# Three start-up edits in a fused attention and SiLU kernel: where a small read is issued, how many warm-up matmuls run, and how a cast is shared

## The chip, the core and the metric

The kernel runs on one core of a Trainium2 chip. A core has five engines that run beside each other: TensorE (PE, matrix products into PSUM), VectorE (DVE), ScalarE (ACT), GpSimd (POOL) and SyncE (SP, which here only issues transfers). Transfers between main memory and the core's SBUF run on 16 DMA engines. They can be issued from SP's queue and ScalarE's queue (hardware queues, q1 and q10 in the profile) and from GpSimd's (the software queue, q0), and only GpSimd's change the element type on the way. The metric is device time in microseconds, the median over runs; lower is better.

## The reference

Inputs are float32. `q`, `k`, `v` have the shape 8 x 8 x 576 x 64 (batch, head, position, feature), `w_in` 512 x 2048 and `w_out` 2048 x 512.

```python
q_s = exp(q - max(q, axis=-1));  q_s /= sum(q_s, axis=-1) + 1e-09     # over features
k_s = exp(k - max(k, axis=2));   k_s /= sum(k_s, axis=2) + 1e-09      # over positions
kv  = einsum('bhsd,bhse->bhde', k_s, v)
x   = einsum('bhsd,bhde->bhse', q_s, kv)      # then heads side by side: 4608 x 512
h   = x @ w_in
out = (h * sigmoid(h)) @ w_out                # 4608 x 512, float32
```

## The kernel before

The 4608 tokens are eight batches of 576 positions. The attention works by batch: q and k go through an exponential on ScalarE, q is divided by its row sums, `kv` is a small product over positions, and `x` is q (transposed) times kv. The two wide products work in chunks of 512 tokens, from chunk 1 on with a scheme that uses seven block products in place of eight. Chunk 0 covers the 576 tokens of batch 0 and is done plainly.

The order of all work is written out by hand. `ORDER` at the top of the file is a list of names; the loop at the end of the kernel calls them one by one, and each engine carries out its own instructions in that order. A scheduler adds the waits that the data need, but moves nothing.

Names that matter here, all in the opening that handles batch 0:

- `touch(i, x, eng)` (line 550) reads 64 single float32 numbers, spread over a large tensor, into a corner of a tile that is used much later. Nothing uses the numbers. It is called for k and v of batch 0 on ScalarE's queue and for `w_in` on GpSimd's (lines 554 to 556), ahead of everything in `ORDER`.
- `heat(n)` (line 561) issues n matmuls of float32 zeros, 128x128 by 128x512, into PSUM bank 5. Nothing uses the result. `heat0` has five and stands ahead of batch 0's first exponential, `heat1` has one and stands between the first transposes (`tr0.0`) and the first kv product (`kv0.0`).
- `lq0.c`, `lk0.c`, `lv0.0`, `lv0.1.g`: the loads of batch 0, on SP. A tile is 128 rows by two heads; half 1 of v comes in two parts, one head pair each.
- `gate` (line 627): a GpSimd copy of one number of k's first tile. Since GpSimd works in order, it holds back what follows, the loads of `w_in`.
- `W1a0`, `W1a1`, `W1b`, `W1c`, `W1d` (line 628, function `load_w1`): `w_in` in four quarters of 512 columns, the first in two parts, float32 to float16 on the way, on GpSimd's queue. `W2a` and so on do the same for `w_out`.
- `eq`, `z`, `n`: exponential, row sum, normalisation of q; `tr`, `tc`: transposes on TensorE and their copies out of PSUM; `ek`: exponential of k; `vc`: cast of v to bfloat16; `kv`, `kc`: the kv product and its normalising copy; `X0.c`, `x0.c`: the product x and its copies out of PSUM.
- `vc0.1a`, `vc0.1b`, `vc0.1c` (line 619): the cast of v's last half for batch 0. GpSimd takes the first part (nine position groups of 64 features); the second part is cut between ScalarE (groups 0 to 4) and VectorE (groups 5 to 8). `kv0.1.1` waits for both.
- `w{f}.0`, `w{f}.1` (line 306): the wide matmuls of chunk 0 for block f of `w_in`'s columns. Blocks 0 to 3 use W1a, blocks 4 to 7 use W1b.

Of the kernel before, what the change touches and what calls it, by code (L numbers as in the profile page):

```python
# [16 lines left out]

ORDER = """
    lq0.0 lq0.1 lk0.0 lv0.0 lk0.1 lv0.1.0 lv0.1.1 gate W1a0 W1a1 W1b W1c heat0 eq0.0.0 z0.0.0 eq0.0.1 z0.0.1 eq0.1
    n0.0 ek0.0 z0.1 tr0.0 vc0.0 heat1 n0.1 tc0.0b kv0.0 tc0.0a kc0.0 tr0.1 ek0.1 vc0.1b X0.0 tc0.1b  # L20
    vc0.1a vc0.1c W1d lq1.0 lq1.1 W2a kv0.1.0 kv0.1.1 kc0.1 tc0.1a x0.0v X0.1 x0.0a x0.1v w0.0 w2.0 w1.0 x0.1a W2b1 lk1.0 w1.1 h1 w0.1 w3.0 w2.1
    W2b2 w3.1 h0 v1 v0 w5.0 w5.1 w4.0 w4.1 h2 v2 h3 w6.0 w6.1 h5 v3 h4 v5 w7.0 w7.1 h7 WS1.1 w9.0 v4 h6 w9.1 WS0.1
    w8.0 w8.1 v7 lk1.1 h9 h8 w11.0 v6 eq1.0.0 w11.1 v9 v8 h11 WS1.2 w10.0 lv1.1 w10.1 v11 w12.0 w12.1 eq1.0.1 W2c1
# [47 lines left out]
def kernel(  # L71
# [9 lines left out]
    nc = tc.nc  # L81
# [4 lines left out]
    J = S // P  # L86
# [463 lines left out]
    def touch(i, x, eng):  # L550
        rows4 = x.rearrange("(a p z) f -> p a z f", a=4, p=16)
        eng.dma_start(out=touched[:, i, :, None], in_=rows4[:, :, 0, 0:1])

    touch(0, k[0].rearrange("h s d -> (h s) d"), nc.scalar)
    touch(1, v[0].rearrange("h s d -> (h s) d"), nc.scalar)
    touch(2, w_in, nc.gpsimd)
    make_identity(nc, ident_f)
    nc.vector.tensor_copy(ident, ident_f)
    nc.vector.memset(vaug[:, :, :, D:E1], 1.0 / XS)
# [24 lines left out]
    def op(name, f, *args):  # L584
        assert name not in ops
        ops[name] = lambda: f(*args)
# [29 lines left out]
    for g in range(2):  # L616
        op(f"lv0.1.{g}", load, 0, "vt", v, 1, nc.sync, g, g + 1)
        op(f"kv0.1.{g}", kv, 0, 1, 6, g, g + 1)
    for x, eng, g, j0, j1 in (("a", nc.scalar, 1, 0, 5), ("b", nc.vector, 1, 5, J), ("c", nc.gpsimd, 0, 0, J)):
        op(f"vc0.1{x}", vcast, 0, 1, eng, g, g + 1, j0, j1)  # L620
    for c, b0, b1 in ((0, 4, 0), (1, 6, 2)):
        op(f"X0.{c}", lambda c=c, b0=b0, b1=b1: (xt_mm(0, c, 0, 320, b0, 0), xt_mm(0, c, 320, 256, b1, 0)))
        op(f"x0.{c}a", xt_evac, 0, c, b0, 0, 320, 0, nc.scalar)
        op(f"x0.{c}v", xt_evac, 0, c, b1, 0, 256, 320, nc.vector)
    for i, n in enumerate((5, 1)):
        op(f"heat{i}", heat, n)
    op("gate", lambda: nc.gpsimd.tensor_copy(gate, st[0]["kt", 0][0:1, 1, 0:1]))
    for x, f, n, c0, c1 in (("W1a0", 0, 4, 0, 2), ("W1a1", 0, 4, 2, 4), ("W1b", 4, 4, 0, 4), ("W1c", 8, 4, 0, 4), ("W1d", 12, 4, 0, 4)):
        op(x, load_w1, f, f + n, c0, c1)
# [67 lines left out]
    for t in range(1, NCH):  # L697
# [6 lines left out]
        for g in range(2):  # L704
            n = f"{t}.{g}."
# [123 lines left out]
```

## Time and profile before

| | |
|---|---|
| median of 3 runs | 256.7 us (256.35 to 260.25) |
| the profiled execution, its own time | 257.51 us |
| its span, first to last instruction | 255.7 us |
| TensorE matmuls busy | 247.9 us, 97% of the span |
| VectorE / ScalarE / GpSimd busy | 205.7 / 190.6 / 66.7 us |
| read from and written to main memory | 36.70 MB and 9.44 MB |
| mean granted TensorE clock | 0.999 of full speed |

All times in the views are microseconds from the start of the span. A row of the order of time gives start, duration, engine, source line, operation, output and inputs with shapes, a count, and in brackets how long the engine sat idle before and what ended that. In the chain that ended last, each row is a start, a duration and what the end was waiting on at that time. In the view of waits a row gives who waited for whom, the total, how often and the longest. A DMA queue's row gives packets, megabytes and the time that its packets took as a share of 16 engines; overlapping packets can bring that over 100%.

### The profile page before, as it was taken

To read this page: it belongs to the slowest core of one execution; us is meant where nothing else is said; L and a number is where in the kernel's file an instruction comes from. 1 tells how busy PE (TensorE), PEld (TensorE's weight loads), DVE (VectorE), ACT (ScalarE), POOL (GpSimd) and SP (SyncE) were. 2 spreads that over 40 slices of the span, in tenths; PEclk is the share of its full clock that TensorE was granted. 3 is DMA by queue.
4 is the path that set the end of the run, shared out by engine and by line. 5 is a ranking of instruction groups with operands and counts; after the bars stand their busy time and mean duration, and the time that the engine had idled before them with its cause. 6 is when DMAs were issued, how large, how long until landed. Compare 5 with 4: busy or idle time off the path is not lost.

```text
span 255.7 us, 6428 instructions
## 1 busy us (share of the span) xinstructions
PE 247.9 (97%) x2712; PEld 204.3 (80%) x2712; DVE 205.7 (80%) x277; ACT 190.6 (75%) x226; POOL 66.7 (26%) x64
## 2 busy tenths in 40 slices
PE   7789999999999999999999999999999999999994
PEld 3367755666888888888888888888888888888883
DVE  3868998899999998998987986896569836886752
ACT  4765867899999999999879979737587666664411
POOL 2563872540360631530083040006000000000022
PEclk9999999999999999999999999999999999999999
DMA  7999999879959947996964950021807000700365
GB/s 231 350 200 298 270 337 328 310 150 382 388 117 242 404 158 181 349 307 165 301 246 87 243 198 3 3 61 24 170 6 160 6 0 4 154 11 3 69 139 124
DMA packets 36205, 45.90 MB, mean 180 GB/s; under 512 B 16448, under 2 KB 21248, under 8 KB 36176
## 3 DMA queue, kind: packets, MB, share of 16 engines
q1 hardware_dynamic: 29424, 33.56, 45.1%
q0 software_dynamic: 6192, 11.60, 17.6%
q10 hardware_dynamic: 560, 0.33, 0.6%
q8 instruction: 21, 0.34, 0.6%
q14 instruction: 8, 0.07, 0.1%
HBM read 36.70 MB, written 9.44 MB: 180 GB/s over the span
## 4 chain that ended last, share of the span: by engine, by line
PE 89%; DMA 7%; DVE 1%; POOL 1%; ACT 1%; SPq 0%; issue 0%; ACTq 0%
PE PS L502 37%; PE PS L424 35%; PE PS L444 5%; PE PS L306 5%; DMA W<-in_moe_w_in_dram 4%; DMA kt<-in_k_dram 3%; PE PS L334 2%; PE PS L247 2%; PE PS L281 2%; DMA out_dram<-ow 1%; POOL W L566 1%; DVE h L144 0%; PE PS L233 0%; SPq L151 0%; DVE ow L763 0%; ACT ow L776 0%
## 5 line engine op out<-in xcount | busy, mean ns | idle before, releaser
L402 DVE TENSOR_TENSOR h<-PS,h 128x1024 f32<-128x1024 f32 (+1 forms) x45 | 54.1, 1205 | 9.5 <-PE PS L424 7.8
L502 PEld LDWEIGHTS <-GT 128*128 128x128 f16 x512 | 50.0, 98 | 6.0
L424 PEld LDWEIGHTS <-WS 128*128 128x128 f16 x480 | 46.6, 98 | 6.8 <-issue 1.0
L408 ACT ACTIVATE GT<-h 128x1024 f16<-128x1024 f32 (+1 forms) x45 | 46.7, 1050 | 0.9 <-DVE h L402 0.8
L502 PE MATMUL PS<-W,GT 128*128 128x256 f16 x384 | 47.2, 273 | 0.0
L424 PE MATMUL PS<-XS,WS 128*128 128x256 f16 (+1 forms) x360 | 45.0, 272 | 0.0
L142 ACT COPY h<-PS 128x1024 f32<-128x1024 f32 (+1 forms) x31 | 31.1, 1003 | 16.9 <-PE PS L424 15.8
L502 PEld LDWEIGHTS <-S 128*128 128x128 f16 x384 | 37.1, 98 | 4.7
L424 PEld LDWEIGHTS <-W 128*128 128x128 f16 x360 | 35.1, 98 | 4.5 <-issue 0.2
L215 POOL TENSOR_TENSOR eq<-eq,rzq 128x1152 bf16<-128x1152 bf16 x13 | 27.7, 2139 | 36.0 <-DVE rzq L210 35.8
L144 POOL CAST vaug<-vt 128x1152 bf16<-128x1152 f32 (+1 forms) x13 | 16.3, 1268 | 61.4 <-DMA vt<-in_v_dram 53.3
L502 PE MATMUL PS<-T,S 128*128 128x256 f16 x256 | 32.0, 273 | 0.0
L424 PE MATMUL PS<-XT,W 128*128 128x256 f16 (+1 forms) x240 | 29.9, 272 | 0.0
L144 DVE COPY h<-PS 128x1024 f32<-128x1024 f32 (+1 forms) x14 | 17.0, 1212 | 8.6 <-PE PS L424 3.7
L162 ACT ACTIVATE eq<-qt 128x1152 bf16<-128x1152 f32 (+1 forms) x19 | 18.8, 1008 | 4.6 <-DMA qt<-in_q_dram 4.6
L781 POOL DMA_DIRECT2D out_dram<-ow x5 | 2.7, 545 | 70.0 <-DVE ow L763 70.0
L167 ACT ACTIVATE ek<-kt 128x1152 bf16<-128x1152 f32 x16 | 18.4, 1161 | 3.3 <-DMA kt<-in_k_dram 3.2
L408 ACT ACTIVATE GT<-PS 128x1024 f16<-128x1024 f32 (+1 forms) x15 | 15.2, 1014 | 6.6 <-PE PS L424 6.5
L206 DVE TENSOR_REDUCE zq<-eq 128x18 f32<-128x1152 bf16 x13 | 17.5, 1346 | 1.2 <-ACT eq L162 0.9
L306 PE MATMUL PS<-XT,W 128*128 128x288 f16 x128 | 16.0, 286 | 0.4 <-DMA W<-in_moe_w_in_dram 0.4
L502 PE MATMUL PS<-T,GT 128*128 128x256 f16 x128 | 16.3, 273 | 0.0
L502 PE MATMUL PS<-W,S 128*128 128x256 f16 x128 | 16.1, 273 | 0.0
(86 smaller groups left out, 332.8 us busy)
## 6 DMA issues: line engine op xcount, KB each, us to landing
out_dram<-ow SPq DMA_DIRECT2D x64, 128.0 KB, 3.3
qt<-in_q_dram SPq DMA_DIRECT2D x12, 576.0 KB, 5.7
kt<-in_k_dram SPq DMA_DIRECT2D x12, 576.0 KB, 7.1
vt<-in_v_dram SPq DMA_DIRECT2D x11, 576.0 KB, 6.9
qt<-in_q_dram POOLq DMA_DIRECT2D x4, 576.0 KB, 11.9
kt<-in_k_dram POOLq DMA_DIRECT2D x4, 576.0 KB, 12.6
vt<-in_v_dram POOLq DMA_DIRECT2D x4, 576.0 KB, 12.1
W<-in_moe_w_in_dram POOLq DMA_DIRECT2D x3, 512.0 KB, 10.4
```

Of the source, the lines that this page charges most:

```text
L142: eng.copy(out=o, in_=i)
L144: eng.tensor_copy(o, i)
L162: nc.scalar.activation(out=half(st[b]["eq"], cc)[:, :, g0:g1], in_=jgd(b, "qt", cc)[:, :, g0:g1], func=ACT.Exp)
L167: nc.scalar.activation(out=half(ek, cc), in_=jgd(b, "kt", cc), func=ACT.Exp)
L206: nc.vector.reduce_sum(out=z, in_=e, axis=AX.X)
L215: eng.tensor_tensor(out=e, in0=e, in1=r[:, :, :, None].to_broadcast([128, J, 2, D]), op=ALU.mult)
L306: nc.tensor.matmul(out=PS[:, WIDE[fb] + n, 0:S // 2], lhsT=W1[:, c, fb * 128:(fb + 1) * 128], rhs=XTS[0][:, c, n * (S // 2):(n + 1) * (S / ...
L402: nc.vector.tensor_tensor(out=four(t, i), in0=group_bank(t, g), in1=four(t, i), op=ALU.add)
L408: nc.scalar.activation(out=group_out(t, f, n), in_=x, func=ACT.Silu, scale=1.0 / XS)
L424: nc.tensor.matmul(out=PS[:, bank + p // 2, (p % 2) * HT:(p % 2) * HT + width(t)], lhsT=a[:, c, p * 128:(p + 1) * 128], rhs=bb[:, c, 0:wid ...
L444: nc.tensor.matmul(out=PS[:, 2 + tb, :], lhsT=GTS[t % 2][:, fc, tb * 128:(tb + 1) * 128], rhs=W2[:, fc, :], start=(fc == 0), stop=(fc == N ...
L502: nc.tensor.matmul(out=PS[:, bank, m * HN:(m + 1) * HN], lhsT=a[:, fc, m * 128:(m + 1) * 128], rhs=bb[:, fc, :], start=(first and fc == 0) ...
```

## The change

Three edits, all in the opening. The small read of `w_in` is issued on ScalarE's queue, as the other two are, and no longer on GpSimd's. `heat0` has three matmuls in place of five, and `heat1` with its one is gone from `ORDER`. Of the last part of v's cast for batch 0, ScalarE takes four position groups in place of five, and VectorE five in place of four.

```diff
-    n0.0 ek0.0 z0.1 tr0.0 vc0.0 heat1 n0.1 tc0.0b kv0.0 tc0.0a kc0.0 tr0.1 ek0.1 vc0.1b X0.0 tc0.1b
+    n0.0 ek0.0 z0.1 tr0.0 vc0.0 n0.1 tc0.0b kv0.0 tc0.0a kc0.0 tr0.1 ek0.1 vc0.1b X0.0 tc0.1b
...
-    touch(2, w_in, nc.gpsimd)
+    touch(2, w_in, nc.scalar)
...
-    for x, eng, g, j0, j1 in (("a", nc.scalar, 1, 0, 5), ("b", nc.vector, 1, 5, J), ("c", nc.gpsimd, 0, 0, J)):
+    for x, eng, g, j0, j1 in (("a", nc.scalar, 1, 0, 4), ("b", nc.vector, 1, 4, J), ("c", nc.gpsimd, 0, 0, J)):
         op(f"vc0.1{x}", vcast, 0, 1, eng, g, g + 1, j0, j1)
...
-    for i, n in enumerate((5, 1)):
-        op(f"heat{i}", heat, n)
+    op("heat0", heat, 3)
```

## The prediction

> **What bounds the kernel now.** I read the chain that ended last first, cut to its first 40 us.
>
> ```profile
> 1.75 6.62 DMA kt<-in_k_dram
> 8.38 0.05 issue
> 8.43 0.18 POOL gate L627
> 8.61 1.43 POOL W L566 x2
> 10.04 9.22 DMA W<-in_moe_w_in_dram
> 19.26 0.05 issue
> 19.31 11.93 PE PS L306 x96
> ```
>
> Until 19.3 us the end is set by transfers. The first k tile lands at 8.38, the gate lets GpSimd issue W1's quarters, and the second quarter (W1b) lands at 19.26. From 19.31 TensorE runs without a hole: the view of waits for TensorE alone names none after that. So whatever moves 19.31 moves the end by as much, and whatever comes earlier counts only if it moves 19.31. TensorE's own order of time shows the opening:
>
> ```profile
> 1.49 6.74 PE L563 MATMUL PS<-h 128*128 128x512 f32 x10 [1.49 <-DVE h L545]
> 8.54 0.66 PE L233 MATMUL PS<-ident,eq 128*128 128x128 bf16 x9 [0.31 <-DVE eq L215]
> 9.04 1.08 PE L563 MATMUL PS<-h 128*128 128x512 f32 x2
> 11.11 0.48 PE L247 MATMUL PS<-vaug,ek 64*64 64x65 bf16 x36 [0.99 <-ACT vaug L142]
> ...
> 12.90 0.95 PE L247 MATMUL PS<-vaug,ek 64*64 64x65 bf16 x36 [0.26 <-POOL vaug L144]
> 14.44 0.44 PE L281 MATMUL PS<-qT,kvn 64*64 64x320 bf16 x8 [0.59 <-DVE kvn L260]
> 14.81 4.09 PE L306 MATMUL PS<-XT,W 128*128 128x288 f16 x32
> 19.31 0.91 PE L306 MATMUL PS<-XT,W 128*128 128x288 f16 x6 [0.40 <-DMA W<-in_moe_w_in_dram]
> ```
>
> Each float32 warm-up matmul is two records, so five are ten. The wide matmuls on W1's first quarter begin at 14.81, end at 18.91, and wait 0.40 for W1b. That 0.40 is the slack in front of all that the change touches.
>
> Last, the small reads, the gate and the last v casts in the order of time of all engines:
>
> ```profile
> 1.33 0.67 POOL L552 DMA_DIRECT2D kvn<-in_moe_w_in_dram  x1 [0.89 <-POOLq L813]
> 1.34 0.43 ACTq L552 DMA_DIRECT2D kvn<-in_v_dram  x1
> ...
> 8.43 0.18 POOL L627 COPY gate<-kt 1x1 f32<-1x1 f32 x1 [5.84 <-DMA kt<-in_k_dram]
> ...
> 12.86 0.47 ACT L142 CAST vaug<-vt 128x320 bf16<-128x320 f32 x1 [0.15 <-DMA vt<-in_v_dram]
> 12.86 0.29 DVE L144 CAST vaug<-vt 128x256 bf16<-128x256 f32 x1 [0.71 <-DMA vt<-in_v_dram]
> ```
>
> **The warm-up.** Three matmuls go, 3 x 2 records. Two follow the third in heat0 (four records of 0.43 us, 6.35 to 8.23); nothing real waits for TensorE before 8.54, where the first transpose waits for VectorE. heat1 fills 9.04 to 10.12, ahead of a 0.99 us wait for ScalarE's cast. Direct gain: 0. What remains is the clock, a rival below. The page's clock row cannot show it (it has no record before the first change); the spacing does: weight loads and records start at 2.50, 3.36, 4.21, 5.06 and 5.92, 0.85 us apart, then at 6.35, 6.78 and 7.21, 0.43 apart. The clock doubled at 5.92, after 4.43 us of unbroken work, inside the third matmul.
>
> **The small read.** GpSimd loses an issue of 0.67 us. Its identity matrix comes 0.67 earlier, but that is first needed at 8.54, and GpSimd then idles 5.84 us before the gate. ScalarE's queue gains a third issue of 0.43 (row at 1.34), ending at about 2.2; its next real work is the first q at 4.57 after 2.33 idle. Hidden, with 1.9 to spare.
>
> Two queues are moved past. The semaphore records show that SP's and ScalarE's transfers share eight completion semaphores in turn, the ninth reusing the first: the last v load waits for the first q tile (landed 4.55). With one more in front, the last but one v load on SP has to wait for that q tile, where it was issued at 3.56, and the last one for the small read of k (landed 4.10) and its turn. That is about 1.0 and 0.4 us later. Their bytes queue behind k's second tile, which lands at 11.38 with the engines full from 3.5 on, so their landings of 12.13 and 12.84 should stand; if not, the first 0.40 is still covered at W1b. GpSimd's transfers have eight of their own: W2's first part no longer follows the small read, and every later pair is the same as before.
>
> What no row shows is W1's first load being the first transfer GpSimd issues at all. From below: 0. From above: the small read was issued at 1.33 and the software queue has no packet before 5.26, 3.93 us; W1's first was issued at 8.55, first packet 11.33, 2.78 us; GpSimd's last stores, into nearly empty engines, took about 1.27 (250.29 to 251.56). So a first use may cost 3.93 - 2.78 = 1.15, at most 3.93 - 1.27 = 2.66. I take 0: the small read's issue of 0.67 is no longer than W1's (0.74 to 0.77), and ScalarE's second read was slow in the same crowd (issued at 1.34, landed at 5.54).
>
> **The v cast.** ScalarE goes from 320 to 256 elements a row. By its rows of 320 (0.468) and 1152 (1.162) an element costs 0.83 ns: 0.415, ending at 13.28 in place of 13.33. VectorE goes from 256 to 320: 0.295 plus 64 elements at 0.5 ns (its 128x128 identity cast took 0.23) to 1.33 ns (512 from PSUM took 0.68): 0.33 to 0.38, ending before 13.24. Behind it VectorE's transpose copy slides 0.09 at most, and VectorE then idles 0.40 before the reciprocal at 13.89. So kv's second half, X0.1 and the wide matmuls come 0.05 earlier (14.76).
>
> **Sum.** W1b still lands at 19.26; the 0.05 lengthens its wait to 0.45. Total 0.0 us: 257.5 against the profiled execution's own 257.51 (span 255.7 and 1.8 around it), which is 0.8 above the median of the runs; on the median 256.7. Its own range, with half a microsecond for the run, is 256.2 to 257.2.
>
> **Rival 1, slower: the clock is not up when the wide matmuls start.** Place: TensorE between 6.4 and 14.8. The third matmul ends 0.4 us after the doubling, so little margin is left if the doubling comes later in a run. After it TensorE idles from 6.35 to 8.54 and from 9.20 to 11.11, with 0.66 us of transposes between. In this trace an idle of 0.99 kept the clock; after the last matmul (252.02) it fell at 255.10, 3.08 later. 2.19 lies between, nearer the fall. It decides once the clock is half beyond 14.4. Price: kv's second half +0.24 and X0.1 +0.44, then half rate until 4.43 us of steady work is done, counted from 12.90 (17.33) or 14.81 (19.24): (17.33 - 14.81)/2 = 1.3 or 4.43/2 = 2.2. Less the 0.40 slack: +1.5 to +2.5, 258.2 to 259.2.
>
> [...] I put 0.22 on it.
>
> **Rival 2, slower: the first transfer on GpSimd's queue is dear.** Place: W1's first load. At 1.15, its packets start at 12.48 and land at 15.67 in place of 14.52; the wide matmuls, 4.09 long, then end at 19.8, +0.5. W1b: the 121 software packets of 11.3 to 12.4 took 87% of the engines, 0.96 us, which partly idle now, so it lands up to 0.96 later. +0.5 to +1.0; I take 257.4. At 2.66 W1b lands as much later, 259.3. It decides from 0.69 at the latest (0.29 between W1's first landing and 14.81, and the slack of 0.40), earlier where engines idle. Chance 0.18.
>
> [...]
>
> **Rival 3, faster: W1b loses its straggler.** In 16.8 to 19.3 the queues held this:
>
> ```profile
> q0 software_dynamic: 504, 0.50, 121.8%
> q8 instruction: 1, 0.02, 2.2%
> ```
>
> One fetch of instructions kept one engine 0.89 us from 17.17. W1b's landing records show 15 engines done by 18.34 and one at 19.26. Removing the warm-up takes 12 instructions from TensorE (two loads, two matmuls each), 12 x 0.062 = 0.74 us at the wide matmuls' pace: the fetch comes near 17.9, still ahead of that engine's last packets (19.26 - 0.89 = 18.37), so its delay stays. If it slips 1.2 us it misses, and the wait of 0.40 goes: 256.3. Chance 0.09.
>
> **How the numbers follow.** No change 0.48 (it includes that the moved read does nothing for W1 either way), rival 1 0.22, rival 2 0.18, rival 3 0.09, something unseen 0.03. Range 256.0 to 259.3: it reaches from just under rival 3 to the upper ends of the two slow ones; a run's own spread and the unseen are the rest. Two per cent (5.1 us) is about what a measurement of this kernel can tell from no change; no case reaches it, so the chances of faster, same and slower are 0.01, 0.96 and 0.03, the last for the unseen.
>
> **What would show it.** Right: six warm-up records with the doubling inside them; ScalarE's cast near 0.42; wide matmuls from about 14.8 with 0.12 us spacing; a wait of about 0.45 for W1; the next 96 from about 19.3. Rival 1: spacing of 0.25 after 14.8. Rival 2: W1's first software packet after 12. Rival 3: no wait for W1 and no lone late engine. A first k tile that lands well off 8.4 would make the forecast wrong through none of these.

## The result, and the profile after

| | before | after |
|---|---|---|
| median of 6 runs each | 256.52 us | 259.15 us |
| lowest to highest | 256.25 to 260.25 | 257.81 to 259.80 |
| ratio of the times, 95% interval | | 1.0101 (1.007 to 1.0132) |
| the profiled execution, own time and span | 257.51 and 255.7 us | 257.81 and 256.0 us |
| mean granted TensorE clock of that execution | 0.999 | 0.993 |

The run of 260.25 us is a slow one and is left out of the ratio. The changed kernel is 2.6 us slower: inside the range, but against a forecast of no change. Its six runs list mean clocks of 0.979, 0.980, 0.980, 0.980, 0.993 and 0.993; the profiled one is the mildest of them in time. TensorE's order of time in the profile after:

```profile
1.49 5.49 PE L563 MATMUL PS<-h 128*128 128x512 f32 x6 [1.49 <-DVE h L545]
8.49 0.66 PE L233 MATMUL PS<-ident,eq 128*128 128x128 bf16 x9 [1.51 <-DVE eq L215]
10.79 0.71 PE L247 MATMUL PS<-vaug,ek 64*64 64x65 bf16 x36 [1.64 <-ACT vaug L142]
11.43 1.14 PE L233 MATMUL PS<-ident,eq 128*128 128x128 bf16 x9
...
14.96 15.97 PE L306 MATMUL PS<-XT,W 128*128 128x288 f16 x128
```

Two idle stretches, of 1.51 and 1.64 us, stand where the three taken-out matmuls were (0.31 and 0.99 us before), and the second set of transposes takes 1.14 us where it took 0.68. The view by stages, cut at the changes of the clock, says why. Its columns are the stretch and its length, then busy time and instructions of TensorE, of its weight loads, of VectorE, ScalarE and GpSimd, then the granted clock, the DMA share and GB/s:

```profile
3.69:7.10 3.41, 3.29 (x4) 0.68 (x3) 1.80 (x4) 2.31 (x3) 0.00 (x0) 1.00 1.04 391
7.10:10.51 3.41, 0.66 (x9) 0.62 (x10) 3.34 (x4) 2.20 (x3) 2.42 (x4) 1.00 1.05 396
10.51:13.93 3.42, 3.14 (x89) 2.68 (x88) 2.31 (x6) 3.25 (x6) 3.02 (x6) 0.50 1.17 240
```

The clock opened at 7.10. The next 3.41 us held 0.66 us of work, and for the 3.41 after that the clock was halved. Here it was back at 13.93, a microsecond before the wide matmuls, so this execution lost little by it. The clock records of the two traces have full-clock stretches of 249.17 us before and of 3.41 and 242.35 us after: 73, 1 and 71 times 3.413. The expectations below call a stretch of this length a window.

That leaves a puzzle. In this execution the last matmul starts at 250.99, where it started at 251.75 before, and yet the span is 0.3 us longer. The loss is behind the last matmul. SP's waits at the very end (L824 before, L823 after, the wait for all stores), with total, count and longest, first before and then after:

```profile
SPq L824 <- DMA out_dram<-ow: 1.0, 3, 0.4
```

```profile
SPq L823 <- DMA out_dram<-ow: 2.2, 1, 2.2
```

And the queues in a window of 2 us that holds the last stores, after; an issue's row ends with the median time to landing:

```profile
q14 instruction: 1, 0.01, 2.8%
issues: line engine op xcount, KB each, median us to landing
out_dram<-ow ACTq DMA_DIRECT2D x1, 64.0 KB, 2.8
out_dram<-ow SPq DMA_DIRECT2D x1, 64.0 KB, 2.9
```

Before, the same window had no instruction fetch, and these stores took 2.0 and 2.1 us. The packet records put an 8 KB fetch, one packet of q14, at 252.69, 0.90 us long. The landing records show what came with it: each of the last three stores has 15 of 16 parts landed by 253.24, 253.74 and 254.03, and one part at 254.36, 254.53 and 254.70. From the start of the last matmul to the start of the last instruction is 3.9 us before and 5.0 after. I call this stretch the end.

The records do not name the DMA engine that carried the fetch; that it is the one of the late parts is inferred from the times.

Two theories stand, then: the clock, halved in the gap behind the warm-up, and a fetch of instructions that has moved into the last stores.

### The profile page after: what moved, and what is told of

Read it like the earlier page. It is cut to its first block, busy times and chain, and to the rows that moved or that the text cites. A ratio compares the mean times of both kernels' runs of the same rounds, so it can differ in the third digit from the quotient of the medians.

```text
span 256.0 us, 6416 instructions
## 1 busy us (share of the span) xinstructions
PE 246.0 (96%) x2706; PEld 204.4 (80%) x2706; DVE 205.2 (80%) x277; ACT 190.7 (74%) x226; POOL 66.4 (26%) x63
## 4 chain that ended last, share of the span: by engine, by line
PE 92%; DMA 4%; ACT 1%; SPq 1%; DVE 0%; issue 0%; ACTq 0%
PE PS L502 37%; PE PS L424 36%; PE PS L306 6%; PE PS L444 5%; DMA vt<-in_v_dram 3%; PE PS L247 2%; PE PS L334 2%; PE PS L281 2%; PE PS L233 1%; DMA out_dram<-ow 1%; SPq L151 1%; ACT vaug L142 0%; DVE ow L762 0%; ACT ow L775 0%; ACT sc L747 0%
```

## Experiments: the warm-up, and the rest without it

**The warm-up edit alone**, on the kernel before.

```diff
-    ... tr0.0 vc0.0 heat1 n0.1 ...
+    ... tr0.0 vc0.0 n0.1 ...
-    for i, n in enumerate((5, 1)):
-        op(f"heat{i}", heat, n)
+    op("heat0", heat, 3)
```

> The kernel before with the warm-up edit alone (three matmuls, then none). Clock theory: after the warm-up opens the clock, TensorE is idle for most of one window of 3.4 us, the clock falls back and comes up only one to three windows later; so this kernel alone gives the whole loss: 258.0 to 260.0 us, mean granted clock 0.979 to 0.993 in most executions. Theory of a dear first transfer on GpSimd's queue, or of SP's late v loads: this kernel keeps the small read on GpSimd, so it stays at 256.0 to 257.0 with clock 0.999.

Measured: 258.42 us against 256.51, ratio 1.0066 (1.0041 to 1.0091), clocks 0.980, 0.980, 0.980 and 0.987. The stages of its profiled execution:

```profile
5.58:9.00 3.42, 1.30 (x11) 0.52 (x9) 3.35 (x5) 2.23 (x3) 0.86 (x2) 1.00 1.04 389
9.00:12.41 3.41, 1.71 (x48) 1.57 (x45) 2.99 (x6) 3.06 (x4) 2.81 (x5) 0.50 1.09 329
12.41:15.82 3.41, 2.82 (x57) 1.81 (x56) 2.05 (x6) 2.32 (x5) 3.41 (x6) 0.50 1.21 196
15.82:19.24 3.42, 3.42 (x16) 2.17 (x15) 0.33 (x1) 0.04 (x1) 1.82 (x3) 0.50 1.24 206
```

The clock opens at 5.58, closes at 9.00 after a stretch with 1.30 us of work, and stays half for three stretches, 10.24 us in all, to 19.24. The wide matmuls start 0.24 us apart until then, 0.12 afterwards. Those beyond the first 32 begin at 21.1, where the next kernel has them at 18.7. The end of the span is unchanged at 3.9 us behind the last matmul. So the clock theory holds, and by itself accounts for some 1.9 us by the medians, 1.7 by the ratio. It is not the opening that fails: the clock came up in time and fell again.

**The read and the cast alone**: the changed kernel with all six warm-ups back.

```diff
-    op("heat0", heat, 3)
+    for i, n in enumerate((5, 1)):
+        op(f"heat{i}", heat, n)
...
-    ... tr0.0 vc0.0 n0.1 ...
+    ... tr0.0 vc0.0 heat1 n0.1 ...
```

> The changed kernel with all six warm-up matmuls back, so the read and the cast alone. Clock theory: clock 0.999, 255.8 to 256.8 us, no slower than before, W1's first software packet within 0.2 us of 2.8 after its issue. Dear first transfer or late v loads: 257.2 to 259.0 with clock 0.999.

Measured: 257.77 us, ratio 1.0050 (1.0032 to 1.0067), clocks 0.996 to 1.000. My clock theory was not all of it: 1.3 us are left with the clock up. (1.9 and 1.3 are together more than the 2.6 of the whole change; two of its six runs list a clock of 0.993, as much as one halved stretch of 3.41 us makes.) Nor is it W1's first transfer. In the changed kernel that was issued at 8.33 and its first software packet ran at 11.25, 2.9 us later, as against 2.8 before; here the packet ran at 11.18. What differs is the end: 4.8 us, with SP waiting

```profile
SPq L824 <- DMA out_dram<-ow: 2.0, 1, 2.0
```

and a fetch 1.66 us behind the last matmul, where before it came 2.60 behind, when the stores' packets were all but done (their last one ended at 2.68).

**Five matmuls, none in the gap**, and **three with the one in the gap**, both on the changed kernel.

```diff
-    op("heat0", heat, 3)
+    op("heat0", heat, 5)
```

> The changed kernel with five matmuls in heat0 and no heat1. If the gap behind the warm-up closes the clock: TensorE works until 8.2, then has only the transposes (0.7 us) until 10.8, so windows that hold little work are rarer: clock 0.999 in most executions and 0.979 to 0.993 in some, 256.2 to 257.5 us. If it is the opening that fails with three matmuls: clock 0.999 in all, 256.0 to 256.8.

```diff
-    op("heat0", heat, 3)
+    for i, n in enumerate((3, 1)):
+        op(f"heat{i}", heat, n)
...
-    ... tr0.0 vc0.0 n0.1 ...
+    ... tr0.0 vc0.0 heat1 n0.1 ...
```

> The changed kernel with three matmuls in heat0 and heat1's one back behind the first transposes. If the gap closes the clock: the least busy window then holds some 1.7 us of work in place of 0.7, so the clock falls back less often than in the changed kernel, 256.3 to 258.0 us. If the opening fails: as slow as the changed kernel, 258.5 to 259.8 with clock 0.98.

Five and none: 258.14 us, ratio 1.0077 (1.0044 to 1.011). Its seven runs fall in two groups: four at clock 1.000 with 257.3 to 258.1 us, three at 0.986 or 0.987 with 259.5 to 259.8. Three and one: 257.64, ratio 1.0040 (1.0026 to 1.0054), ten runs of 257.1 to 258.4, no slower where the clock is listed as 0.990 to 0.996 than at 1.000 (in the profiled one, 0.996, it fell at 253.2, behind the last matmul). That is the level of the kernel with all six. So the one matmul in the gap is worth more than the two at the end of `heat0`. How much work the stretch behind the opening held, in the profiled executions:

| kernel | stretch behind the opening | TensorE's work in it | clock afterwards |
|---|---|---|---|
| after | 7.10 to 10.51 | 0.66 us, 19% | half |
| warm-up edit alone | 5.58 to 9.00 | 1.30 us, 38% | half |
| three and one | 7.44 to 10.86 | 1.89 us, 55% | full |
| five and none | 7.70 to 11.11 | 2.29 us, 67% | full |
| before | 5.92 to 9.33 | 3.10 us, 91% | full |

The rows of that view for the least busy stretch of the three that kept the clock, in the order three and one, five and none, before:

```profile
7.44:10.86 3.42, 1.89 (x47) 1.19 (x47) 3.35 (x4) 2.69 (x3) 3.02 (x5) 1.00 1.06 393
7.70:11.11 3.41, 2.29 (x49) 1.40 (x47) 3.34 (x4) 2.75 (x3) 3.06 (x5) 1.00 1.05 393
9.33:12.75 3.42, 2.31 (x55) 1.12 (x53) 2.72 (x6) 3.04 (x4) 2.79 (x4) 1.00 1.09 323
```

Where the matmuls run out, two more stretches bear on it: behind 1.66 us of work (49%) from 250.04 in five and none the clock stayed up, behind 1.26 us (37%) from 249.79 in three and one it fell.

The clock opens at 5.21 (four more on ScalarE) to 7.70 us (five and none), and in four kernels with the same six warm-ups at 5.21, 5.43, 5.92 and 7.03. That one kernel, too, is cut differently from run to run is inferred from this, since each has one trace. It would fit five and none coming out both ways, but no trace of one of its half-clock runs is on record. An estimate from the last row: without the 0.79 us of `heat1` that lie in it, 1.5 us would be left, 45%, between the 38% after which it closed and the 49% after which it stayed up.

## Experiments: the end

**No small read of w_in at all**, with six warm-ups and the cast edit. The numbers that the read brings are used by nothing, so only its instruction and its transfer go.

```diff
-    touch(2, w_in, nc.scalar)
```

> Six warm-ups, the cast edit, and no small read of w_in at all (the read's numbers are used by nothing): ScalarE has as many instructions as before, GpSimd one transfer fewer. Theory of ScalarE's extra instruction (it brings a fetch of instructions forward into the last stores): the end from the last matmul to the end of the span is back from 4.6 to 5.0 us to 3.9, the fetch starts 2.5 us or more behind the last matmul, 256.2 to 256.9 us. Rival, GpSimd's missing instruction shifts the fetch: the end stays 4.6 or more, 257.3 to 258.1. Rival, the read does something for W1 that ScalarE's queue does not give it: the end is 3.9, but W1's quarters land later than in the kernel with the read on ScalarE, 257.3 or more.

Measured: 256.62 us, ratio 1.0010 (1.0000 to 1.0021), end 3.9 us, fetch 2.61 behind the last matmul. The end is as it was although GpSimd has one instruction fewer, and W1 does not miss the read: its first software packet runs at 11.33, 3.0 us behind its issue, and the wide matmuls start at 14.5.

**One more ScalarE instruction**, on the kernel before, the read on GpSimd where it was.

```diff
     touch(2, w_in, nc.gpsimd)
+    nc.scalar.activation(out=dummy, in_=dummy, func=ACT.Exp)
```

> The kernel before, the read on GpSimd as it was, with one more tiny ScalarE instruction at the start (the exponential of one number, a second time; it changes nothing that is used). Theory of ScalarE's extra instruction: the end lengthens from 3.9 to between 4.5 and 5.0 us, the fetch starts about 1.7 us behind the last matmul, and the median is 257.2 to 257.8. Rival, the read's place is what costs: as before, 256.2 to 256.8, end 3.9.

Measured: 256.94 us, ratio 1.0022 (1.0010 to 1.0035), end 4.28 us, fetch 1.92 behind the last matmul. The direction is that of the theory and the size is below my numbers. The fetch starts 0.26 us later than in the kernel with read and cast, took 0.37 us in place of 0.72, and the last store landed 3.41 behind the last matmul in place of 3.52. That is 0.1 of the 0.5 us by which the two ends differ; the rest lies behind the landing and is taken up below the table. Why one transfer brings the fetch further forward than one activation, the profile does not show.

**The cast edit alone**, on the kernel before.

```diff
-    (("a", nc.scalar, 1, 0, 5), ("b", nc.vector, 1, 5, J), ...
+    (("a", nc.scalar, 1, 0, 4), ("b", nc.vector, 1, 4, J), ...
```

> The kernel before with the cast edit alone. Both theories: ScalarE's cast 0.41 us in place of 0.47, VectorE's 0.33 to 0.5, no change of the whole: 256.2 to 256.9 us. If the cast carries part of the loss of read and cast together (1.26 us, of which the longer end explains about 0.9): 256.8 to 257.0.

Measured: 256.66 us against 256.46, ratio 1.0014 (1.0005 to 1.0024). ScalarE's cast took 0.415 us, VectorE's 0.49, and from the landing of v's last part to the first wide matmul it was 1.92 us where it had been 1.98. So the edit does in its place what was forecast, 0.05 us. That the whole comes out 0.2 us slower is at the edge of what was resolved; the two other kernels that have the cast edit and an undisturbed end (no read of w_in, 1.0010, and v's read left out, 1.0003) do not repeat it clearly, and it stays open.

**The read on ScalarE, v's small read left out**, so that ScalarE has as many instructions as before (on the kernel with six warm-ups).

```diff
-    touch(1, v[0].rearrange("h s d -> (h s) d"), nc.scalar)
     touch(2, w_in, nc.scalar)
```

> Six warm-ups, the cast edit and w_in's small read on ScalarE's queue, but v's small read is left out (its numbers are used by nothing), so that ScalarE has as many instructions as before. Theory that the number of ScalarE's instructions times the last fetch: the end is 3.9 us, the fetch starts 2.5 us or more behind the last matmul, 256.3 to 256.9 us. Rival, that it is w_in's read in that queue itself: the end stays 4.6 to 5.0, 257.3 to 258.0.

Measured: 256.53 us against 256.56, ratio 1.0003 (0.9991 to 1.0015), end 3.9, fetch 2.69 behind. w_in's read on ScalarE's queue costs nothing as such. This kernel has as many transfers on the two hardware queues as before, too, so it does not tell the count of ScalarE's instructions from the count of these transfers.

**Four more ScalarE instructions**, on the kernel before.

```diff
     touch(2, w_in, nc.gpsimd)
+    for _ in range(4):
+        nc.scalar.copy(out=dummy, in_=dummy)
```

> The kernel before with four more tiny ScalarE instructions at the start (copies of one number onto itself). One gave a fetch 1.92 us behind the last matmul in place of 2.6 and an end of 4.28. Theory of the fetch's place: it comes earlier still, near the last matmul or ahead of it, where the last stores have not begun; the end is then 3.9 to 4.2 again and the time 256.3 to 256.9. Rival, that more instructions simply cost more: the end is 4.6 or more, 257.3 or more.

Measured: 256.49 us against 256.56, ratio 0.9996 (0.9984 to 1.0007), end 3.9. Four more are not dearer here: the fetch starts 0.53 us behind the last matmul. Before, the last two stores are issued 0.8 and 0.9 us behind it. SP's last wait, with one extra, then with four:

```profile
SPq L825 <- DMA out_dram<-ow: 1.1, 1, 1.1
```

```profile
SPq L826 <- DMA out_dram<-ow: 0.9, 3, 0.4
```

All kernels together, ordered by when the fetch starts; landings, too, are counted from the start of the last matmul. ScalarE's instructions are counted as the trace has them, its transfers and waits among them:

| kernel | ScalarE | GpSimd | fetch behind the last matmul | last store landed | end |
|---|---|---|---|---|---|
| v's read left out | 323 | 118 | 2.69 us | 3.04 us | 3.9 us |
| no read of w_in | 323 | 118 | 2.61 | 3.04 | 3.9 |
| before | 323 | 119 | 2.60 | 3.03 | 3.9 |
| warm-up edit alone | 323 | 119 | 2.59 | 3.03 | 3.9 |
| cast edit alone | 323 | 119 | 2.56 | 3.03 | 3.9 |
| one more on ScalarE | 324 | 119 | 1.92 | 3.41 | 4.3 |
| after | 324 | 117 | 1.70 | 3.71 | 5.0 |
| five and none | 324 | 117 | 1.66 | 3.59 | 4.9 |
| read and cast | 324 | 117 | 1.66 | 3.52 | 4.8 |
| three and one | 324 | 117 | 1.49 | 3.31 | 4.6 |
| four more on ScalarE | 327 | 119 | 0.53 | 3.04 | 3.9 |

In these eleven traces the fetch goes with ScalarE's count. GpSimd's is 117 in kernels with the fetch at 1.49 to 1.70 and 119 in kernels with it at 0.53 to 2.60, and TensorE's 12 instructions fewer in the warm-up edit alone leave it at 2.59. That it fetches ScalarE's instructions is inferred from this. In all eleven it starts 0.7 to 1.1 us behind the 320th of ScalarE's instructions: the one behind its last store where it has 323, the issue of that store where it has 324, the issue of the store before where it has 327. Where it started 1.49 to 1.92 us behind the last matmul, the last store landed 0.3 to 0.7 us late; where it started at 0.53 or at 2.56 to 2.69, the last store landed at 3.03 or 3.04. The last store packet of before ended at 2.7.

The late store is not the whole of the longer end. From the last landing to the end it is 0.9 us in seven kernels and 1.3 us in four: after, five and none, read and cast, three and one. These four have one transfer more on the hardware queues than before. In the semaphore records the 120 such transfers of before take eight semaphores in turn, and the last store has the eighth; after, there are 121, and the last store has the first. The records of SP's waits show the rest. Before, the wait for the last store is the last of nine, and SP goes on 0.07 us behind it. After, it is the second, done at 254.74, and the seven waits behind it, all of them met by 254.53, take 0.06 us each. That makes 0.4 us, which one more ScalarE instruction without a transfer does not have. So of the 0.7 to 1.1 us by which the end is longer in these four kernels, 0.3 to 0.7 is the late store and 0.4 the order of SP's waits.

A kernel that beats both did not come out of this: those with an undisturbed end and a full clock are at the level of before.

## Why the prediction was wrong

- **The bound and the cover** were read rightly from the trace of before: W1b's landing at 19.26 ahead of a TensorE without holes, and 0.40 us of slack. In the kernel with v's read left out, too, TensorE waits 0.42 us for W1b at 19.01, and for nothing else behind it. But the slack is that of an execution, not of the kernel: in the traces of the cast edit alone and of four more on ScalarE W1b landed at 18.45 and 18.41, and the wide matmuls run from 14.66 and 14.68 without a gap.
- **"Direct gain: 0" for the warm-up** was right about the work taken out. What failed is the weight of rival 1, which was named, placed and priced at +1.5 to +2.5. The warm-up edit alone gave +1.9. It had a chance of 0.22, and a mean clock lower than in any run of before is listed for all six runs of the changed kernel (0.979 to 0.993) and all four of the edit alone (0.980 to 0.987). The step at fault is the comparison of single idle stretches (0.99 kept, 2.19 here, 3.08 fell). In these traces the clock goes with the work in a whole stretch of 3.41 us: behind stretches with 19, 37 and 38% it fell, behind those with 49, 55, 67, 68 and 91% it stayed up. By that measure the trace of before had its least busy stretch at 2.31 us (9.33 to 12.75), 68%, while the gap that the change leaves, from 6.35 to 11.11 with 0.66 us of work, is longer than a whole stretch.
- **"Hidden, with 1.9 to spare" for the third issue on ScalarE** was right at its place and wrong for the kernel. The same text counted TensorE's 12 instructions for what their absence does to a fetch, and did not count ScalarE's one. That one instruction, at 1.8 us, went with a fetch at the other end of the kernel 0.9 us earlier, among the last stores, and with a last store 0.7 us late (0.3 to 0.7 in the four kernels with the transfer). With one more activation and no transfer it came 0.7 us earlier, and the last store 0.4 us late. The transfer's place in the turn of the semaphores, which the prediction followed through the opening alone, went with 0.4 us more in SP's last waits. Together the end is 0.7 to 1.1 us longer, 0.9 of the 1.3 that read and cast cost together; the remaining 0.4 stays open.
- **That 259.15 lies inside the range is partly luck.** The range reached so far up for rivals 1 and 2, each by itself. What happened is rival 1's loss and, at the end of the kernel, one that no rival had.
- **Rival 2** did not happen: 2.9 us to W1's first packet in place of 2.8, of which 0.1 is the issue itself (0.87 us in place of 0.76, in all six kernels in which GpSimd issues nothing ahead of W1). **Rival 3** did not either: in the changed kernel's window from 16.8 to 19.3 the fetch is still there, and W1b's last part lands at 18.95 with 15 of 16 by 17.95. The fetch started at 16.90, though, a little ahead of the 17.17 of before; the shift to 17.9 that was worked out from TensorE's 12 instructions did not show.

```profile
q0 software_dynamic: 504, 0.50, 121.5%
q8 instruction: 1, 0.02, 2.4%
```

- **The v cast**: ScalarE's 0.415 as forecast; VectorE's 0.33 to 0.38 was mis-sized, it took 0.49. It ended behind ScalarE's for that, but in the cast edit alone the chain behind it still gained 0.05 us.

```profile
12.56 0.41 ACT L142 CAST vaug<-vt 128x256 bf16<-128x256 f32 x1 [0.17 <-DMA vt<-in_v_dram]
12.56 0.49 DVE L144 CAST vaug<-vt 128x320 bf16<-128x320 f32 x1 [0.52 <-DMA vt<-in_v_dram]
```

- **SP's late v loads** came as described: the last two were issued from 4.51 in place of 3.56, and their last parts landed at 11.80 and 12.54, no later than before.

## What to carry to other kernels

Here a matmul whose result nobody uses was worth 1.5 us: the changed kernel ran at 259.15 us, with the one in the gap back at 257.64. Before taking such a matmul out, cut the trace into stretches of the length that its clock records show, here 3.41 us, and see how much work the emptiest would keep. And look at both ends of the kernel for what one more instruction does: after, ScalarE's third issue ran at 1.79 us, ahead of 2.29 us in which ScalarE waited for q, but a fetch at the end started 1.70 us behind the last matmul in place of 2.60, and the last store landed 0.7 us late. A transfer more counts there as well: the last store had the first semaphore of the turn in place of the eighth, and SP's last waits took 0.4 us longer.

## What the runs showed that I had not expected

- With one instruction more on ScalarE at the start the last store landed 0.3 to 0.7 us late, with four more no later. The fetch of 8 KB took 0.37 to 0.90 us in the five kernels with a late store. After, SP's wait for the last store ended at 254.74, behind its 16th part at 254.70, where 15 had landed by 254.03.
- Nine waits at the end of the kernel, of which the one that takes long is the second and not the last, went with an end 0.4 us longer.
- With the clock open, a stretch of 3.41 us with 1.30 us of work (38%, the warm-up edit alone, 5.58 to 9.00) was followed by half clock. As to its opening: in five and none the stretch from 0.87 to 4.28 held 2.79 us of work (82%) and the clock opened only at 7.70, one stretch of 3.42 us full of work later; in three and one it opened at 7.44 behind 2.94 us (86%, 4.03 to 7.44).
- Once closed it stayed so for 3.41 us after, where a stretch with 3.14 us of work (92%) ended with the clock open at 13.93, a microsecond before the wide matmuls. In the warm-up edit alone it stayed so for 10.24 us: behind stretches with 1.71 and 2.82 us (50% and 83%) it was still half, and it opened behind one with 3.42 us, full of the wide matmuls.
